# Constants of the start-up laid on another engine, and a key cast held in the order of the text

## The chip, the cores and the metric

The kernel runs on one NeuronCore of a Trainium2 chip. The metric is the device time of one execution in microseconds (us); each median is of a series of 4 to 6 executions (11 or 12 for the kernel before in the experiments). "TensorE", "VectorE", "ScalarE" and "Pool" (GpSimd) appear in profile lines as PE (PEld for its weight loads), DVE, ACT and POOL; SPq is the queue of SyncE, the engine that issues most DMAs (124 of the 151 issues listed for the kernel before). "Granted clock" is the share of full speed that the profile records for TensorE's clock.

## The reference, cut to what matters

A chunked attention feeds a gated feed-forward layer.

```python
# q, k, v: 4 batches, 8 heads, 768 tokens, 64 wide; 8 memory tokens per head
for c in range(24):                         # chunks of 32 tokens
    keys = memory keys + k[32c-16 : 32c+40] # clipped to the sequence
    out[chunk] = softmax(q[chunk] @ keys.T / 8) @ (the same rows of v)
x = out as (3072 tokens, 512)
result = (relu(x @ w_gate) * (x @ w_val)) @ w_out      # 512 -> 1536 -> 512
```

## The kernel before: the parts that matter

The 3072 tokens are worked in eight blocks of 384. Blocks 0 and 1 ("start blocks") are loaded by Pool's queue with a cast on the way and turned on TensorE. Blocks 2 to 7 ("later blocks") are loaded in f32 by SP's queue, cast by VectorE, ScalarE and Pool, and turned by DMA. Each block's feed-forward work consists of twelve "units" (gate and value matmuls, a relu on ScalarE, a product `gvT` on VectorE) and three output units. Attention work of a block is interleaved with the feed-forward units of the block before. In profile lines kf and kn are the loaded and the cast keys, qz the queries, s_ps the scores, v_ps the attention's values, g_ps and vl_ps the gate and value results of the feed-forward.

A scheduler places the instructions of each engine. `pin` keeps an instruction where the text has it among the other pinned ones; an instruction that is not pinned may be moved. The start-up, up to the end of block 1's attention, is chained in the order of the text as well, but only the instructions written there.

```python
pin = tc.keep_in_program_order
...
class LaterBlock(Block):
    def pieces(self, dma):                    # the loads of one block, issued by SP in this order
        def k01():
            ...                               # (memory values first)
            dma(self.kf[16:24, 3], self.mem(mem_k, 0, H, D))
            dma(self.kf[:, 0], self.rows(k, 0, H, self.kbase, 128, D))
        def k12():
            dma(self.kf[0:16, 3], self.rows(k, 0, H, self.kbase + 384, 16, D))
            for t in (1, 2):
                dma(self.kf[:, t], self.rows(k, 0, H, self.kbase + 128 * t, 128, D))
    ...
    def cast_k(self):
        if self.n < 2 + NSTART:
            nc.gpsimd.memset(self.kn[96:128, :, 3], 0.0)          # padding
        view = self.kf.rearrange("p t (a x) d -> p a t (x d)", x=2)
        pin(nc.vector.tensor_copy(self.kn[:, :, 0:3], view[:, :, 0:3]))
        nc.vector.tensor_copy(self.kn[0:24, :, 3], view[0:24, :, 3])   # the tail cast: 24 rows, not pinned
...
# start: first loads, constants by Pool, clearing by ScalarE
b0.load("k", 0); b0.load("q", 0)
...
make_identity(nc, ids["b"])
b0.load("v", 0)
...
lows["first"] = build_low("low_first", NMEM - 16)   # each: memset, two selects, memset, all on Pool
lows["int"] = build_low("low_int", NMEM)
b0.load("k", 4)
...
for u in range(9):                            # block 0's feed-forward, units 0 to 8
    dff[0][u]()
fills = {0: dff[0][9], 1: dff[0][10], 2: dff[0][11]}
start_attention(b1, attention(b1, order0), lambda i: fills.get(i, lambda: warm(2))())
in_text_order(text0)
sp_after(0, w_out_sb[0:1, 0, 0:1])            # SP waits here for the first piece of w_out
for f in b2.pieces(sp):                       # only then are block 2's loads issued
    f()
...
prepare(b2, (hooks, 5), (hooks, 6), (hooks, 7), (hooks, 8))   # b2.cast_k belongs after unit 5 of block 1
```

The softmax here doesn't subtract the row's maximum and nothing guards it: scores larger than these inputs give would overflow.

## Time and profile before

| | before |
|---|---|
| time, median (range) of 4 runs | 265.19 us (264.62 to 265.4) |
| span of the profiled run | 263.3 us |
| TensorE busy | 236.1 us, 90% |
| first gate matmul of block 0 / 1 / 2 (timeline) | 26.44 / 70.94 / 106.68 us |

The page of the kernel before. The first line is busy time and its share of the span; the others give the busy share (or the granted TensorE clock) in tenths of full, for 40 equal slices of 6.6 us.

```profile
PE 236.1 (90%) x1718; PEld 141.7 (54%) x1718; DVE 138.6 (53%) x357; ACT 114.4 (43%) x224; POOL 63.7 (24%) x120
...
PE   5788990398899699999999999999999999999994
...
PEclk9589996579999999999999999999999999999999
```

From the fifteenth slice on TensorE is full. The zero in the seventh slice is a hole. The waits view of the first 60 us says who waited for whom (total, times, longest):

```profile
ACT kb L261 <- DVE kb L257: 15.3, 2, 13.3
...
DVE kn_103 L323 <- DMA kf_99<-in_k_dram: 12.7, 1, 12.7
PE g_ps L431 <- DVE gvT L440: 11.3, 1, 11.3
```

TensorE's 11.3 us and ScalarE's 13.3 us are both waits for VectorE, and VectorE itself waits 12.7 us for a load of keys. The timeline shows the order of events (start, duration, engine, line, operation, destination and source; in brackets the idle time before it and what ended it):

```profile
42.41 0.73 SPq L89 DMA_DIRECT2D here<-w_out_sb  x1
...
44.38 3.37 SPq L89 DMA_DIRECT2D kf_99<-in_k_dram  x4
...
49.38 0.49 DVE L323 CAST kn_103<-kf_99 24x512 bf16<-24x512 f32 x1 [12.71 <-DMA kf_99<-in_k_dram]
49.80 1.00 DVE L440 TENSOR_TENSOR gvT<-vl_ps,g_relu 128x384 f16<-128x384 f32 x2
50.39 1.44 PE L431 MATMUL g_ps<-xT,w_gate_sb 128*128 128x384 f16 x4 [11.26 <-DVE gvT L440]
```

The 24-row tail cast of block 2 stands in front of two products of block 0. Its rows are loaded only after the first piece of w_out is there (42.41 us). VectorE stood for 12.71 us until the cast's rows were there; the two products that the scheduler put behind it start right after it, at 49.80 us. The products read results of TensorE (vl_ps), for which the program has four buffers, shared with g_ps; the next gate matmul waited 11.26 us for a product, and TensorE stopped.

The windows view gives for each stretch its length, busy time and instructions of PE, PEld, DVE, ACT and POOL, then granted clock, DMA share and GB/s. The stretch behind the hole runs at about half clock (0.54 granted):

```profile
39.10:50.40 11.30, 0.04 (x3) 0.06 (x2) 1.02 (x3) 0.00 (x0) 5.57 (x20) 0.62 1.16 212
50.40:55.90 5.50, 5.50 (x28) 2.65 (x28) 2.40 (x5) 2.15 (x5) 0.00 (x0) 0.54 1.08 246
```

The granted clock fell from 1.00 to 0.50 at 41.8 us, 2.7 us after the end of TensorE's last matmul (39.1).

That the tail cast stands so early was the scheduler's choice. In the text it comes right behind the main key cast of the same block, which is pinned. In VectorE's timeline the main cast runs 30 us after its tail, with 35 other instructions of VectorE between them:

```profile
79.48 0.95 DVE L322 CAST kn_103<-kf_99 128x1536 bf16<-128x1536 f32 x1
```

### The profile page before, as it was taken

To read this page: it belongs to the slowest core of one execution; us is meant where nothing else is said; L and a number is where in the kernel's file an instruction comes from. 1 tells how busy PE (TensorE), PEld (TensorE's weight loads), DVE (VectorE), ACT (ScalarE), POOL (GpSimd) and SP (SyncE) were. 2 spreads that over 40 slices of the span, in tenths; PEclk is the share of its full clock that TensorE was granted. 3 is DMA by queue.
4 is the path that set the end of the run, shared out by engine and by line. 5 is a ranking of instruction groups with operands and counts; after the bars stand their busy time and mean duration, and the time that the engine had idled before them with its cause. 6 is when DMAs were issued, how large, how long until landed. Compare 5 with 4: busy or idle time off the path is not lost.

```text
span 263.3 us, 4699 instructions
## 1 busy us (share of the span) xinstructions
PE 236.1 (90%) x1718; PEld 141.7 (54%) x1718; DVE 138.6 (53%) x357; ACT 114.4 (43%) x224; POOL 63.7 (24%) x120
## 2 busy tenths in 40 slices
PE   5788990398899699999999999999999999999994
PEld 3556550165665354556456645664666466546641
DVE  5357920335545842489438934893488258604410
ACT  6436330145535343557246615561565166323321
POOL 8984374315000012134400403052003000000000
PEclk9589996579999999999999999999999999999999
DMA  5599999980006999999969975996699611121012
GB/s 72 72 173 204 204 196 205 249 157 1 2 0 121 232 202 229 229 246 154 165 190 257 140 172 164 248 179 160 171 221 167 171 40 31 32 81 42 0 40 81
DMA packets 96929, 37.55 MB, mean 143 GB/s; under 512 B 78410, under 2 KB 93834, under 8 KB 96906
## 3 DMA queue, kind: packets, MB, share of 16 engines
q1 hardware_dynamic: 85202, 29.85, 53.1%
q0 software_dynamic: 11632, 7.34, 19.3%
q8 instruction: 13, 0.21, 0.3%
q14 instruction: 10, 0.08, 0.1%
q10 hardware_dynamic: 72, 0.07, 0.1%
HBM read 30.43 MB, written 6.29 MB: 139 GB/s over the span
## 4 chain that ended last, share of the span: by engine, by line
PE 75%; DMA 13%; POOL 5%; DVE 2%; issue 2%; ACT 1%; SPq 1%; POOLq 0%; DVEq 0%
PE out_ps L450 24%; PE g_ps L431 21%; PE vl_ps L435 21%; DMA w_gate_sb<-in_moe_w_gate_dram 5%; DMA w_out_sb<-in_moe_w_out_dram 4%; PE s_ps L368 4%; PE o_ps L386 3%; DMA kf_99<-in_k_dram 2%; DMA qT<-qn_105 2%; PE v_ps L282 1%; POOL w_gate_sb L92 1%; SPq L89 1%; POOL w_val_sb L92 1%; POOL qn_105 L92 1%; DVE qz_98 L357 1%
## 5 line engine op out<-in xcount | busy, mean ns | idle before, releaser
L431 PE MATMUL g_ps<-xT,w_gate_sb 128*128 128x384 f16 x384 | 79.5, 330 | 12.0 <-DVE gvT L440 11.3
L440 DVE TENSOR_TENSOR gvT<-vl_ps,g_relu 128x384 f16<-128x384 f32 x96 | 52.9, 554 | 65.9 <-PE vl_ps L435 63.8
L435 PE MATMUL vl_ps<-xT,w_val_sb 128*128 128x384 f16 x384 | 79.3, 329 | 0.1
L438 ACT ACTIVATE g_relu<-g_ps 128x384 f16<-128x384 f32 x96 | 47.0, 490 | 42.8 <-DVE gvT L440 23.7
L450 PE MATMUL out_ps<-w_out_sb,gvT 128*128 128x512 f16 x288 | 64.1, 379 | 0.0
L431 PEld LDWEIGHTS <-w_gate_sb 128*128 128x128 f16 x384 | 36.3, 98 | 31.7 <-issue 13.3
L435 PEld LDWEIGHTS <-w_val_sb 128*128 128x128 f16 x384 | 37.8, 99 | 25.5 <-issue 1.5
L450 PEld LDWEIGHTS <-gvT 128*128 128x128 f16 x288 | 28.0, 98 | 32.0
L453 ACT COPY o_sb<-out_ps 128x512 f32<-128x512 f32 x24 | 14.1, 585 | 51.1 <-PE out_ps L450 50.6
L391 DVE TENSOR_TENSOR x_big<-o_ps,rinv 96x256 f16<-96x256 f32 x64 | 26.5, 417 | 1.5
L368 PE MATMUL s_ps<-qz_97,kb 128*128 128x192 bf16 x64 | 11.5, 258 | 4.1 <-DVE qz_97 L357 2.0
L304 POOL COPY vf_101<-memv 8x512 f32<-8x512 f32 x12 | 7.8, 684 | 23.8 <-DMA memv<-in_mem_v_dram 23.8
L389 DVE RECIPROCAL rinv<-o_ps 96x4 f32<-96x4 f32 x64 | 10.8, 171 | 5.1 <-PE o_ps L386 5.0
L368 PEld LDWEIGHTS <-kb 128*128 128x128 bf16 x128 | 10.6, 100 | 5.0 <-issue 3.0
L368 PE MATMUL s_ps<-qz_98,kb 128*128 128x192 bf16 x64 | 10.8, 244 | 2.0 <-DVE qz_98 L275 0.9
L340 POOL CAST vb_107<-vf_102 128x512 f16<-128x512 f32 x4 | 3.0, 745 | 36.1 <-DMA vf_102<-in_v_dram 36.1
L498 PE MATMUL warm_ps<-idle 128*128 128x256 f16 x38 | 7.9, 337 | 1.2 <-DVE idle L478 1.2
L261 ACT COPY kb<-k_ps 128x240 bf16<-128x240 bf16 x4 | 1.4, 358 | 17.3 <-DVE kb L257 15.3
L323 DVE CAST kn_103<-kf_99 24x512 bf16<-24x512 f32 x3 | 1.3, 421 | 12.7 <-DMA kf_99<-in_k_dram 12.7
L340 POOL CAST vb_108<-vf_102 128x512 f16<-128x512 f32 x4 | 3.1, 772 | 19.4 <-DMA vf_102<-in_v_dram 19.4
L340 POOL CAST vb_109<-vf_102 128x512 f16<-128x512 f32 x4 | 3.0, 743 | 19.2 <-PE vl_ps L435 17.9
L304 POOL COPY vf_102<-memv 8x512 f32<-8x512 f32 x12 | 7.4, 653 | 0.0
(172 smaller groups left out, 234.9 us busy)
## 6 DMA issues: line engine op xcount, KB each, us to landing
out_dram<-o_sb SPq DMA_DIRECT2D x24, 256.0 KB
qf<-in_q_dram SPq DMA_DIRECT2D x6, 768.0 KB
vf_101<-in_v_dram SPq DMA_DIRECT2D x12, 240.0 KB
vf_102<-in_v_dram SPq DMA_DIRECT2D x12, 240.0 KB
kf_99<-in_k_dram SPq DMA_DIRECT2D x9, 256.0 KB
kf_100<-in_k_dram SPq DMA_DIRECT2D x9, 256.0 KB
w_out_sb<-in_moe_w_out_dram POOLq DMA_DIRECT2D x3, 512.0 KB, 11.6
w_gate_sb<-in_moe_w_gate_dram POOLq DMA_DIRECT2D x2, 512.0 KB, 12.0
```

Source lines behind the costliest of these rows:

```text
L304: pin(nc.gpsimd.tensor_copy(self.vf[0:NMEM, j], memv[self.b]))
L340: pin(nc.gpsimd.tensor_copy(self.vb[:, j, :, 0:D], self.vf[:, j]))
L368: nc.tensor.matmul(s_ps[:, i], lhsT=blk.kb[:, 2 * g + i, j, :], rhs=blk.qz[:, 2 * g + i, :, :, 32 * j:32 * j + 32], start=True, stop=not o ...
L389: nc.vector.reciprocal(rinv, o_ps[0:QB, :, D:D + 1])
L391: nc.vector.tensor_tensor(out=x_big[:, 256 * g:256 * g + 256].rearrange("p (h d) -> p h d", h=4), in0=o_ps[0:QB, :, 0:D], in1=rinv_b, op=A ...
L431: nc.tensor.matmul(g_ps, lhsT=w_gate_sb[:, f, 128 * m:128 * m + 128], rhs=blk.xT[:, f, :], start=(f == 0), stop=(f == NFC - 1))
L435: nc.tensor.matmul(vl_ps, lhsT=w_val_sb[:, f, 128 * m:128 * m + 128], rhs=blk.xT[:, f, :], start=(f == 0), stop=(f == NFC - 1))
L438: nc.scalar.activation(g_relu, g_ps, ACT.Relu)
L440: nc.vector.tensor_tensor(out=state["gvT"][:, m].rearrange("p t j c -> p j t c"), in0=vl_ps.rearrange("p (j t c) -> p j t c", j=NJ, t=NT), ...
L450: nc.tensor.matmul(out_ps, lhsT=state["gvT"][:, m, t].rearrange("p j c -> p (j c)"), rhs=w_out_sb[:, m, :], start=(m == 0), stop=(m == NDC ...
L453: nc.scalar.copy(o_sb, out_ps)
L498: nc.tensor.matmul(ps[:, 0:256], lhsT=idle[:, 0:128], rhs=idle, start=True, stop=True)
```

## The change

Its stated intent: start the first loads sooner by taking constants off Pool (VectorE lays the memsets, Pool keeps a few selects between its DMA issues), and hold the key cast and padding of later blocks in the order of the text. The core of the diff:

```diff
-    def build_low(name, first):
-        t = wpool.tile([128, 128], BF16, name=name)
-        nc.gpsimd.memset(t, 0.0)
+    def build_lows(name, first, n, step):          # several masks in one tile, one pair of selects
+        t = wpool.tile([128, n, 128], BF16, name=name)
+        nc.vector.memset(t, 0.0)
 ...
+    def build_ident():                             # memset on VectorE, one select on Pool
 ...
         def cast_k(self):
             if self.n < 2 + NSTART:
-                nc.gpsimd.memset(self.kn[96:128, :, 3], 0.0)
+                pin(nc.vector.memset(self.kn[96:128, :, 3], 0.0))
             view = self.kf.rearrange("p t (a x) d -> p a t (x d)", x=2)
             pin(nc.vector.tensor_copy(self.kn[:, :, 0:3], view[:, :, 0:3]))
-            nc.vector.tensor_copy(self.kn[0:24, :, 3], view[0:24, :, 3])
+            pin(nc.vector.tensor_copy(self.kn[0:24, :, 3], view[0:24, :, 3]))
 ...
-    clear_other_heads(nc.scalar.copy, qz_t[0])     # now two VectorE memsets read as f32
-    b0.cast_mem(nc.vector)
+    b0.cast_mem(nc.scalar.copy)
 ...                                                # b0's second half is loaded earlier,
                                                    # memory rows are issued by SP, not ScalarE
     weights(1024, 1536)
+    clear_other_heads(qz_t[1])
+    lows["last"], = build_lows("low_last", NMEM + 8, 1, 0)
+    sels[1] = build_sel(1, steps)
+    b1.cast_mem(nc.vector.tensor_copy)
     for h0 in (0, 4):                              # block 1's loads now stand behind the selections
         for which in "kqv":
             b1.load(which, h0)
 ...
-    sels[1] = build_sel(1, steps)
-    lows["last"] = build_low("low_last", NMEM + 8)
-    clear_other_heads(nc.vector.tensor_copy, qz_t[1])
-    b1.cast_mem(nc.vector)
```

More of the change, by code (lines that the diff above doesn't have):

```diff
@@ L5 @@
 from concourse import mybir
-from concourse.masks import make_identity
 from concourse._compat import with_exitstack
@@ L128, in build_mask @@
         return mp
-    def build_low(name, first):
-        t = wpool.tile([128, 128], BF16, name=name)
-        nc.gpsimd.memset(t, 0.0)
+    def build_lows(name, first, n, step):
+        t = wpool.tile([128, n, 128], BF16, name=name)
+        nc.vector.memset(t, 0.0)
         for base, mult in ((-first, 1), (first + 55, -1)):
             nc.gpsimd.affine_select(
-                out=t, in_=t, pattern=[[mult, 128]], compare_op=ALU.is_ge,
+                out=t, in_=t, pattern=[[-step * mult, n], [mult, 128]], compare_op=ALU.is_ge,
                 fill=LOW, base=base, channel_multiplier=-32 * mult)
-        nc.gpsimd.memset(t[:, 0:NMEM], 0.0)
-        return t
+        nc.gpsimd.memset(t[:, :, 0:NMEM], 0.0)
+        return [t[:, i] for i in range(n)]
     def build_chunks():
         t = wpool.tile([128, 2, NT, 32], BF16, name="chunks")
-        nc.gpsimd.memset(t, 1.0)
+        nc.vector.memset(t, 1.0)
         for base, mult in ((0, 1), (31, -1)):
@@ L148, in build_chunks @@
                 fill=0.0, base=base, channel_multiplier=-32 * mult)
+        return t
+    def build_ident():
+        t = wpool.tile([128, 128], BF16, name="ident_b")
+        nc.vector.memset(t, 0.0)
+        nc.gpsimd.affine_select(out=t, in_=t, pattern=[[-1, 128]], compare_op=ALU.not_equal,
+                                fill=1.0, base=0, channel_multiplier=1)
         return t
@@ L169, in shifted @@
                            ap=[steps.ap[0], [-1, KR]] + mids + [[1, BAND]])
-        nc.vector.memset(sel[:, :, :, 0:NMEM], 0.0)
+        sl = sel[:, :, :, 0:NMEM]
+        nc.vector.memset(sl, 0.0)
         nc.vector.tensor_copy(sel[:, :, first:first + 3, NMEM:], shifted(rel[first], [[QB, 3]]))
         nc.vector.tensor_copy(sel[:, :, odd, NMEM:], shifted(rel[odd], []))
-        sl = sel[:, :, :, 0:NMEM]
         nc.gpsimd.affine_select(
@@ L226, in load_mem, with cast_mem @@
                 dma(dst, self.mem(m, 0, H, KR * D))
-        def cast_mem(self, engine):
+        def cast_mem(self, copy):
             for dst, src in zip((self.kc, self.vc), self.mems):
-                engine.tensor_copy(dst[0:TOK0], src)
+                copy(dst[0:TOK0], src)
         def keys(self, h):
@@ L478 @@
     nc.vector.memset(idle, 0.0)
-    b0.load("k", 0)
-    b0.load("q", 0)
-    for b in (b0, b1):
-        b.load_mem(nc.scalar.dma_start)
-    scratch = wpool.tile([1, 1], F32, name="scratch")
-    nc.scalar.activation(scratch, zeros[0:1], ACT.Exp)
-    def clear(op, t, ps, x):
-        z = zeros[ps]
-        op(t[ps, :, x], bass.AP(tensor=z.tensor, offset=z.offset, ap=[z.ap[0], [0, HP], [0, NT], [0, 128]]))
-    def clear_other_heads(op, t):
-        clear(op, t, slice(0, D), 1)
-        clear(op, t, slice(D, 128), 0)
-    clear_other_heads(nc.scalar.copy, qz_t[0])
     def warm(n):
@@ L500, with clear_other_heads @@
     warm(16)
-    ids["b"] = wpool.tile([128, 128], BF16, name="ident_b")
-    make_identity(nc, ids["b"])
-    b0.load("v", 0)
+    b0.load("k", 0)
+    for b in (b0, b1):
+        b.load_mem(nc.sync.dma_start)
+    scratch = wpool.tile([1, 1], F32, name="scratch")
+    nc.scalar.activation(scratch, zeros[0:1], ACT.Exp)
+    ids["b"] = build_ident()
+    b0.load("q", 0)
+    b0.load("v", 0)
+    b0.load("k", 4)
+    b0.cast_mem(nc.scalar.copy)
+    ids["chunks"] = build_chunks()
+    lows["first"], lows["int"] = build_lows("low_first", NMEM - 16, 2, 16)
+    b0.load("q", 4)
+    def clear_other_heads(t):
+        nc.vector.memset(t[0:D, :, 1].bitcast(F32), 0.0)
+        nc.vector.memset(t[D:128, :, 0].bitcast(F32), 0.0)
     steps = build_steps()
+    clear_other_heads(qz_t[0])
+    b0.load("v", 4)
+    ids["h"] = wpool.tile([128, 128], F16, name="ident_h")
+    nc.vector.tensor_copy(ids["h"], ids["b"])
     for t in vb_t:
@@ L508 @@
         nc.vector.memset(t[:, :, QB:128], 0.0)
-    b0.cast_mem(nc.vector)
-    ids["chunks"] = build_chunks()
-    lows["first"] = build_low("low_first", NMEM - 16)
-    lows["int"] = build_low("low_int", NMEM)
-    b0.load("k", 4)
-    ids["h"] = wpool.tile([128, 128], F16, name="ident_h")
-    nc.vector.tensor_copy(ids["h"], ids["b"])
     order = [(j, g) for j in range(NJ) for g in range(2)]
@@ L563, in start_attention, with selections @@
         fill(6)
-    def rest_of_b0():
-        b0.load("q", 4)
+    def selections():
         sels[0] = build_sel(0, steps)
-        b0.load("v", 4)
         weights(0, 256)
         weights(256, 512)
-    start_attention(b0, attention(b0, order0), lambda i: (warm(2), rest_of_b0() if i == 1 else None))
+    start_attention(b0, attention(b0, order0), lambda i: (warm(2), selections() if i == 1 else None))
     weights(512, 1024)
     weights(1024, 1536)
+    clear_other_heads(qz_t[1])
+    lows["last"], = build_lows("low_last", NMEM + 8, 1, 0)
+    sels[1] = build_sel(1, steps)
+    b1.cast_mem(nc.vector.tensor_copy)
     for h0 in (0, 4):
```

## The prediction

> **What bounds the kernel now.** From 106.7 us to the end TensorE is the limit: the windows view gives it 152.4 us of work in 156.6, and its longest wait there is 0.6 us. The idle time lies before. The largest piece is one hole: the timeline has TensorE idle for 11.26 us up to 50.39 us, waiting for a VectorE product (gvT). The cause is one instruction ahead of it in VectorE's stream: the 24-row tail of block 2's key cast (kn_103 from kf_99), which waits 12.71 us for a key load. That load is issued only after the first w_out piece lands (42.4 us); the cast starts at 49.4 and is not needed until about 80. It was not pinned, and the scheduler put it after the seventh gvT of block 0. The hole costs twice: the granted clock is 0.54 from 50.4 to 55.9, so four gate matmuls took 1.44 us instead of 0.65. [...]
>
> **What the change does.**
> 1. Tail cast and padding are pinned. In the changed order the cast stands behind six gvT of block 1. The hole closes: -11.3 us. The stretch 50.4 to 55.9 then runs at full clock; adding up its chain (four matmul groups of 0.65, a query turn of 0.5) I estimate 3.4 us instead of 5.5: -2.1 us.
> 2. Pool's start. Pool loses the identity memset (1.21 us), chunks memset (0.28), two low memsets (0.20 each) and two selects (0.29 to 0.36 each). VectorE gains these memsets (0.1 to 0.3 each) and head clearing (about 1.6, an estimate from the 232-word memset's 0.25); ScalarE gains the memory casts and loses its clearing (2.93). Weights are issued earlier (about 11 instead of 12.4 us). Queries are issued later (3.5 instead of 2.2) but should land about when they did (7.9). TensorE's start hangs on the first key load (issued 1.37, landed 6.8), unchanged; block 0's attention is then a chain of small steps, not of loads. Value: -0.3 us, uncertain by 1.
> 3. Block 1's loads now stand behind selections that need VectorE after block 0's attention: issued near 28 us instead of 18.9. Weights occupy the queue until about 31 anyway, and block 1 first needs its keys at 38.5: no cost.
> 4. The tail cast now delays block 2's key turn by about 0.5 us, where TensorE already waited 2.0 us (scores for qz_97, 88.0); two output matmuls now go ahead of them. Net +0.2. Later blocks: +0.3 at most.
>
> **Sum.** 265.08 - 11.3 - 2.1 - 0.3 + 0.4 = 251.8; I put 251.5 us, range 249.0 to 254.5 (8 in 10). Faster by over 2%: 0.97; within 2%: 0.02; slower: 0.01.
>
> **What would show it.** No TensorE wait over 3 us after 10 us, clock 1.00 from about 17 us on; the tail cast at about 65 us without a wait for a load; block 1's feed-forward from about 57 instead of 70.9 us; first weight issue near 11; first scores still near 10.4.
>
> **What would make it wrong.** A second wait under the hole: block 1's late loads arriving after 39 us, or block 2's keys after about 65. ScalarE's casts of memory rows (about 4 us) delaying its first key copies. Pinned casts holding up gvT in every later block.

The sum came to 251.8 us, put at 251.5, and its -2.1 us for the half clock rests on the trace of the kernel before (granted clock 0.54, a gate group of 1.44 us). Durations of work that the kernel before does not contain are estimates: VectorE's memsets there took 0.06 to 0.25 us, and ScalarE's clearing of 3072 elements a row took 2.93 us, which gives 3.9 for casts of 2x2048 (measured after: 1.90 and 1.89 us).

## The result, and the profile after

The changed kernel takes 250.7 us (median of 4 runs, 250.43 to 252.49) against 265.19 us. The ratio is 0.9471, with a 95% interval of 0.9425 to 0.9518. A ratio here is always the mean time of one kernel's runs over that of the other's of the same rounds, so it is not quite the ratio of the medians quoted.

| | before | after |
|---|---|---|
| time, median | 265.19 us | 250.7 us |
| span of the profiled run | 263.3 us | 249.1 us |
| first gate matmul of block 0 | 26.44 | 26.12 |
| block 0's to block 1's first gate matmul | 44.50 us | 30.82 us |
| block 1's to block 2's first gate matmul | 35.74 us | 35.68 us |
| from there to the end | 156.62 us | 156.48 us |

The differences of the three stages come from the same timeline starts as in the table before. One stage holds 13.68 of the 14.2 us. The page after, the same lines:

```profile
PE 234.6 (94%) x1718; PEld 140.8 (57%) x1718; DVE 138.2 (55%) x363; ACT 115.2 (46%) x224; POOL 60.0 (24%) x110
...
PE   5788999889979999999999999999999999999994
...
PEclk9999999999999999999999999999999999999999
```

TensorE's busy time is the same within 1.5 us; its idle time fell. The waits view of TensorE, whole span:

```profile
PE s_ps L374 <- DVE qz_97 L363: 1.8, 1, 1.8
PE s_ps L374 <- DVE qz_97 L281: 1.7, 2, 1.0
PE k_ps L250 <- POOL low_first L135: 1.7, 1, 1.7
```

The longest wait is now 1.8 us, the one before block 2's first scores. The timeline where the hole was, and where the tail cast went:

```profile
38.52 0.82 PE L437 MATMUL g_ps<-xT,w_gate_sb 128*128 128x384 f16 x4
...
44.61 0.70 SPq L88 DMA_DIRECT2D here<-w_out_sb  x1
...
46.23 4.62 SPq L88 DMA_DIRECT2D kf_99<-in_k_dram  x4
...
65.98 0.96 DVE L328 CAST kn_103<-kf_99 128x1536 bf16<-128x1536 f32 x1
66.85 0.41 DVE L329 CAST kn_103<-kf_99 24x512 bf16<-24x512 f32 x1
```

The gate group that stood at 50.39 us now starts at 38.52 and takes 0.82 instead of 1.44 us. The loads did not come sooner: SP's wait for w_out ended at 44.61 us, 2.2 us later than before. The keys were late in both; after the change nothing stands behind them.

The windows view of the stretch where the hole was and of the one behind it:

```profile
39.10:50.40 11.30, 10.07 (x116) 7.05 (x115) 6.22 (x16) 6.33 (x15) 4.05 (x17) 1.00 1.20 206
50.40:55.90 5.50, 4.57 (x62) 3.87 (x61) 3.56 (x12) 3.17 (x8) 0.95 (x2) 1.00 0.78 214
```

The clock row needs care: it reads 1.00 from the first microsecond after the change (the trace holds no clock record before 13.94 us), yet the first key turn (16 transposes at 6.49 us) took 0.97 us where the same turn takes 0.59 at 38.00 us, and the query turn behind it (7.93 us) took 0.85. In the kernel before a query turn took 0.85 us at 7.90, where the granted clock was 0.50 (8 to 10 us), and 0.53 at 16.57, where it was 1.00. So I take it that the array was at half clock at the start after the change too, and trust the durations of equal matmuls more than this row.

### The profile page after: what moved, and what is told of

Read it like the earlier page. It is cut to its first block, busy times and chain, and to the rows that moved or that the text cites. A ratio compares the mean times of both kernels' runs of the same rounds, so it can differ in the third digit from the quotient of the medians.

```text
span 249.1 us, 4702 instructions
## 1 busy us (share of the span) xinstructions
PE 234.6 (94%) x1718; PEld 140.8 (57%) x1718; DVE 138.2 (55%) x363; ACT 115.2 (46%) x224; POOL 60.0 (24%) x110
## 4 chain that ended last, share of the span: by engine, by line
PE 85%; DVE 5%; ACT 3%; POOL 2%; DMA 2%; issue 2%; POOLq 0%; DVEq 0%; ACTq 0%
PE out_ps L456 25%; PE g_ps L437 23%; PE vl_ps L441 23%; PE s_ps L374 5%; PE v_ps L288 3%; PE o_ps L392 3%; DMA qT<-qn_105 2%; PE s_ps L378 1%; DVE x_big L397 1%; DVE kb L263 1%; PE k_ps L250 1%; DVE gvT L446 1%; POOL kn_103 L91 1%; ACT qz_98 L280 1%; ACT qz_97 L280 1%
## 5 line engine op out<-in xcount | busy, mean ns | idle before, releaser
L437 PE MATMUL g_ps<-xT,w_gate_sb 128*128 128x384 f16 x384 | 78.2, 326 | 0.7 <-ACT xT L411 0.7
L441 PE MATMUL vl_ps<-xT,w_val_sb 128*128 128x384 f16 x384 | 78.4, 326 | 0.0
L310 POOL COPY vf_101<-memv 8x512 f32<-8x512 f32 x12 | 7.5, 662 | 26.2 <-DMA memv<-in_mem_v_dram 19.5
L382 ACT ACTIVATE ex_110<-s_ps 128x384 f16<-128x384 f32 x8 | 3.9, 491 | 7.1 <-PE s_ps L374 4.9
L310 POOL COPY vf_102<-memv 8x512 f32<-8x512 f32 x12 | 7.1, 628 | 0.0
L356 DVE COPY kb<-kT 128x1440 bf16<-128x1440 bf16 x6 | 3.2, 536 | 7.0 <-DMA kT<-kn_103 4.5
```

The costliest lines, as they stand in the source:

```text
L310: pin(nc.gpsimd.tensor_copy(self.vf[0:NMEM, j], memv[self.b]))
L437: nc.tensor.matmul(g_ps, lhsT=w_gate_sb[:, f, 128 * m:128 * m + 128], rhs=blk.xT[:, f, :], start=(f == 0), stop=(f == NFC - 1))
L441: nc.tensor.matmul(vl_ps, lhsT=w_val_sb[:, f, 128 * m:128 * m + 128], rhs=blk.xT[:, f, :], start=(f == 0), stop=(f == NFC - 1))
```

## The experiments

Theory: the one unpinned tail cast stood ahead of products that TensorE needed, and cost 11.3 us of waiting plus about 2 us of half clock (0.54 granted over the 5.5 us behind the hole). First rival: the start, with constants off Pool and earlier issues, earned the time. Second rival: block 2's loads as such were the limit, and moving the cast only moves the wait. All kernels below gave correct results.

### Only the pins, only the tail's pin, and only the start

`pins_only` is the kernel before with both pins; `tail_pin_only` with the tail's alone; `start_only` is the changed kernel with both taken back.

```diff
 # pins_only, on the kernel before (tail_pin_only: the second pair of lines alone)
-                nc.gpsimd.memset(self.kn[96:128, :, 3], 0.0)
+                pin(nc.vector.memset(self.kn[96:128, :, 3], 0.0))
-            nc.vector.tensor_copy(self.kn[0:24, :, 3], view[0:24, :, 3])
+            pin(nc.vector.tensor_copy(self.kn[0:24, :, 3], view[0:24, :, 3]))
 # start_only: the reverse of these, on the changed kernel
```

> The kernel before with nothing but the two pinned instructions of the key cast (tail cast, and padding memset on VectorE). Theory (the unpinned tail cast at VectorE's head blocks TensorE, and the idle array then runs at half clock): 251.8 us, 13.4 below before, no TensorE wait over 3 us after 10 us. Rival (the earlier issues at the start earn the time): about 264.5, hole still there.

> The changed kernel with the two instructions unpinned again, all start changes kept. The order listing puts the tail cast behind the eleventh gvT of block 0, later than before (seventh). Theory: a smaller hole at a later place, about 5 to 6 us of TensorE idle ending near 51 us when the tail rows land, plus some 2 us of half clock: 258.5 us (256.5 to 260.5). Rival (the start earns the time): about 251.

> The kernel before with only the tail cast pinned; the padding memset stays unpinned on Pool. Theory (the tail cast alone makes the hole): the same as with both pins, ratio to before 0.952 within 0.005, no TensorE wait over 3 us after 10 us. Rival (the padding memset on Pool has a share): clearly above 0.957.

> The changed kernel once more, as the mark of this call: 250.5 to 252.5 us, as its two earlier series.

| run | median | ratio to before (95%) | block 0's to block 1's first gate matmul |
|---|---|---|---|
| before, same chip | 265.81 us | 1 | 44.50 us (the profile above) |
| `pins_only` | 253.11 | 0.952 (0.9475 to 0.9565) | 30.82 us |
| `tail_pin_only` | 252.16 | 0.9491 (0.9472 to 0.951) | 30.83 us |
| `start_only` | 259.4 | 0.9772 (0.9745 to 0.9799) | 39.50 us |
| `after_third` (the changed kernel) | 251.46 | 0.947 (0.9443 to 0.9498) | 30.82 us |

The tail's pin alone shortens the stage to what the whole change does, within 0.01 us. Where the hole was, TensorE now works, and the tail cast stands without a wait behind the main one:

```profile
37.66 0.82 PE L431 MATMUL g_ps<-xT,w_gate_sb 128*128 128x384 f16 x4
...
65.49 0.41 DVE L323 CAST kn<-kf 24x512 bf16<-24x512 f32 x1
```

The median of `tail_pin_only` is 0.7 us above that of the changed kernel, but the intervals overlap, so the rest of the change is not resolved from nothing. The first rival falls as the source of the gain.

`start_only` was predicted at 258.5 and took 259.4 us: the scheduler placed the unpinned cast in a different place (behind the eleventh product), and the hole moved with it. Its timeline:

```profile
51.18 0.53 DVE L329 CAST kn<-kf 24x512 bf16<-24x512 f32 x1 [9.39 <-DMA kf<-in_k_dram]
51.63 0.67 DVE L291 CAST vb<-v_ps 128x512 f16<-128x512 f32 x1
...
52.35 0.38 PE L392 MATMUL o_ps<-vb,ex 128*128 128x66 f16 x4 [6.94 <-DVE vb L291]
52.54 1.47 PE L437 MATMUL g_ps<-xT,w_gate_sb 128*128 128x384 f16 x4
```

The wait of TensorE is 6.94 us instead of 11.26, because it had more work to do before it ran into the cast; the half clock behind it is there again (1.47 us for a gate group, granted clock 0.50 from 50.4 to 55.9 us). The start's changes alone had pushed the cast later by four products, as a side effect of where the scheduler then put it; that is most of the gain `start_only` shows: the stage gives 5.00 (39.50 instead of 44.50 us) of the 6.1 us between the two profiled spans. The other 1.05 us is an earlier first gate matmul (25.39 instead of 26.44), which lies within the scatter of the start (see "Why the prediction was right").

`pins_only` was 1.3 us above its mark. Its profile has the same 30.82 us stage; the excess lies elsewhere: its start was late (block 0's first gate matmul at 27.46 us), and the stage from block 1's to block 2's first gate matmul took 37.32 instead of 35.7 us, because the array ran at half clock there for 3.4 us (0.78 and 0.88 granted over the two windows of 5 us below). The granted clock falls at 77.8 us, 1.5 us after the only wait of TensorE in that stretch, 1.8 us before block 2's scores; that this wait caused it is inferred from the order. Its windows and timeline there:

```profile
75.00:80.00 5.00, 3.76 (x24) 1.93 (x24) 3.87 (x11) 1.85 (x4) 0.00 (x0) 0.78 1.02 235
80.00:85.00 5.00, 5.00 (x41) 2.78 (x40) 1.88 (x9) 1.76 (x4) 0.61 (x1) 0.88 1.03 197
```

```profile
76.24 0.49 PE L368 MATMUL s_ps<-qz,kb 128*128 128x192 bf16 x4 [1.77 <-DVE qz L357]
...
78.27 3.11 PE L450 MATMUL out_ps<-w_out_sb,gvT 128*128 128x512 f16 x7
```

Seven output matmuls took 3.11 us; the same seven took 1.67 after the change, behind an equally long wait (1.78 us). In `tail_pin_only` that stage was as long (37.26 us), behind waits of 0.66 and 1.17 us; in the kernel before, a wait of 1.99 us at the same scores was followed by full clock (1.00 granted from 55.5 us to the end). What decides is not shown. For comparing kernels it is scatter of some 1.6 us.

### The wait without the half clock

`hole_filled` keeps the cast where it was and gives TensorE needless matmuls in the hole.

```diff
-    fills = {0: dff[0][9], 1: dff[0][10], 2: dff[0][11]}
+    def busy(n):                       # writes a score tile that nobody reads
+        ps = sps.tile([128, 2, 2, NT, 32], F32, name="s_ps")
+        for _ in range(n):
+            nc.tensor.matmul(ps[:, 0], lhsT=idle[:, 0:128], rhs=idle[:, 0:192], start=True, stop=True)
+    def busy_and_unit():
+        busy(125)
+        dff[0][9]()
+    fills = {0: busy_and_unit, 1: dff[0][10], 2: dff[0][11]}
```

> The kernel before with 125 needless matmuls (192 columns, about 10 us) on TensorE where the hole is; the tail cast stays where it was. It separates the two costs of the hole. Theory (11.3 us of waiting and 2.1 us of half clock afterwards): the wait stays, the stretch behind it takes 3.4 instead of 5.5 us, total 263.1 us. If the half clock costs nothing: 265.2. If the clock were the larger part: under 260.

Measured: 263.6 us, ratio 0.9924 (0.9893 to 0.9955). The timeline:

```profile
37.89 10.49 PE L620 MATMUL s_ps<-idle 128*128 128x192 f16 x125
...
48.48 0.41 DVE L323 CAST kn<-kf 24x512 bf16<-24x512 f32 x1 [12.98 <-DMA kf<-in_k_dram]
...
49.42 0.81 PE L431 MATMUL g_ps<-xT,w_gate_sb 128*128 128x384 f16 x4 [1.04 <-DVE gvT L440]
```

The cast still waits 12.98 us, but the gate group behind it takes 0.81 instead of 1.44 us. The stage took 42.61 instead of 44.50 us: the half clock cost 1.89 us, and the other 11.79 of the 13.68 us are left for the wait. So the half clock is measured on its own, and the wait by subtraction. (In this run block 0's first gate matmul came 1.06 us earlier than in the profile of before and the cast 0.90 us earlier, so up to 0.2 us of the wait may belong to the clock.) Kept busy, the array did not drop: the granted clock was 1.00 from 39.1 to 50.4 and from 50.4 to 55.9 us, where the kernel before had 0.62 and 0.54.

### The same hole closed from the other end

`tail_rows_early` leaves the cast unpinned and loads the 24 rows of block 2 at the start, ahead of SP's wait for w_out.

```diff
+            def tail():                                    # taken out of k01 and k12
+                dma(self.kf[16:24, 3], self.mem(mem_k, 0, H, D))
+                dma(self.kf[0:16, 3], self.rows(k, 0, H, self.kbase + 384, 16, D))
+            if self.n > 2: ...                             # later blocks: first of their pieces
+            else: tail()                                   # block 2: at once
 ...
+    b2_pieces = b2.pieces(sp)
     sp_after(0, w_out_sb[0:1, 0, 0:1])
-    for f in b2.pieces(sp):
+    for f in b2_pieces:
```

> The kernel before, tail cast unpinned, but the 24 tail rows of block 2's keys are loaded at the start, ahead of the wait for w_out. The scheduler then places the cast in block 0's attention, with its data there. Theory (only the cast's wait for its rows matters, whichever end is moved): about 251.8 us, no hole. Rival (the load traffic of block 2 as a whole has to be waited for): 260 or more, the wait turning up at the main key cast.

Measured: 252.18 us, ratio 0.9486 (0.9462 to 0.9511), stage 30.92 us; no wait of TensorE above 2.2 us. The cast stands early and waits for nothing:

```profile
17.54 0.38 DVE L332 CAST kn<-kf 24x512 bf16<-24x512 f32 x1
```

The remaining key loads of block 2 came as late as ever and nothing waited for them. So the second rival falls too: what counted was that one instruction's data came after its turn, and either end could be moved.

### Block 1's loads, later by the change

After the change block 1's loads stand behind two Pool selections that need VectorE. `loads_first` puts them back in front.

```diff
-    clear_other_heads(qz_t[1])
-    lows["last"], = build_lows("low_last", NMEM + 8, 1, 0)
-    sels[1] = build_sel(1, steps)
-    b1.cast_mem(nc.vector.tensor_copy)
     for h0 in (0, 4):
         ...                                      # block 1's loads and w_out
+    clear_other_heads(qz_t[1])
+    ...                                          # the same four, here
```

> The changed kernel again, as the mark for the runs of the same call: 250.7 us.

> The changed kernel with block 1's loads issued before the selections that wait for VectorE, as they stood before the change. The changed kernel's queue runs dry between 29 and 32 us because these loads are issued at 30.5. Theory (off the critical path): the dry stretch goes, w_out and block 2's keys land 3 to 4 us earlier, the time stays within 0.4 us of the changed kernel. Rival (the late loads cost part of the gain): over 0.8 us faster.

Measured on one chip: 252.17 us for the changed kernel (ratio 0.9487, 0.9449 to 0.9526) and 251.4 for `loads_first` (0.9463, 0.9437 to 0.9488). The medians differ by 0.8 us, more than the 0.4 expected; the intervals overlap, and the stage from block 0 to block 1 is 30.82 us in both profiles. (The same reordering puts `best` 0.85 us ahead of `scores_later` below. No stage of the profiles shows such a gain, but a small one is not excluded.) The effect on the queue is plain. Windows of the changed kernel (first series), then of `loads_first`; the last two columns are DMA share and GB/s:

```profile
30.00:32.00 2.00, 2.00 (x14) 1.17 (x12) 1.95 (x5) 0.55 (x2) 2.00 (x5) 1.00 0.14 21
```

```profile
30.00:32.00 2.00, 2.00 (x14) 1.22 (x13) 1.86 (x4) 0.55 (x2) 0.24 (x1) 1.00 1.51 190
```

The queue runs nearly dry for some 3 us after the change, and SP's wait for w_out ends at 40.51 us in `loads_first` instead of 44.61, 46.83 and 45.01 us in the three profiles of the changed kernel. TensorE is busy for all 2.00 us of that window in both, so the gap in the loads was no loss to it.

The same pair shows why Pool was so late. Pool's timeline in the changed kernel, then in `loads_first`:

```profile
27.20 1.96 POOL L135 TENSOR_SCALAR_AFFINE_SELECT low_last<-low_last 128x128 bf16<-128x128 bf16 x2 [10.11 <-DVE sel_499 L177]
29.21 1.06 POOL L138 MEMSET low_last<- 128x8 bf16 x1
29.31 1.19 POOL L180 TENSOR_SCALAR_AFFINE_SELECT sel_499<-sel_499 114x128 f16<-114x128 f16 x1
```

```profile
33.40 0.67 POOL L135 TENSOR_SCALAR_AFFINE_SELECT low_last<-low_last 128x128 bf16<-128x128 bf16 x2
34.12 0.10 POOL L138 MEMSET low_last<- 128x8 bf16 x1
34.22 0.41 POOL L180 TENSOR_SCALAR_AFFINE_SELECT sel<-sel 114x128 f16<-114x128 f16 x1
```

From the first start to the last end these four instructions take 3.3 us in one place and 1.2 in the other. In the first place VectorE runs two casts of f32 memory rows (1.21 and 1.30 us, 27.79 to 30.23). In the other place no such cast runs beside them (there they end at 29.92 us). So the 128x8 memset took 1.06 us beside a cast and 0.10 without. What makes it slower is not shown, and the notes of `prof` call spans on Pool rough.

It also puts a number of the prediction in doubt. The identity's memset and select cost Pool 1.21 and 1.15 us before, and I booked the memset as Pool's own work. The timeline of before has VectorE's memory casts beside them for nearly all of that time:

```profile
2.79 1.24 DVE L230 CAST kn_103<-kf_99 2x2048 bf16<-2x2048 f32 x1 [0.61 <-DMA kf_99<-in_mem_k_dram]
2.97 1.21 POOL masks.py:197 MEMSET ident_b<- 128x128 bf16 x1
...
3.96 1.29 DVE L230 CAST vc_122<-vf_101 2x2048 f16<-2x2048 f32 x1
4.25 1.15 POOL masks.py:199 TENSOR_SCALAR_AFFINE_SELECT ident_b<-ident_b 128x128 bf16<-128x128 bf16 x1
```

After the change, with those casts on ScalarE, the select takes 0.30 us:

```profile
2.29 0.30 POOL L153 TENSOR_SCALAR_AFFINE_SELECT ident_b<-ident_b 128x128 bf16<-128x128 bf16 x1
```

### Warming the array longer

```diff
-    warm(16)
+    warm(36)
```

> The changed kernel with 36 instead of 16 warming matmuls at the start, so that TensorE is busy until the first keys land (about 6.5 us). In the changed kernel the first key turn takes 0.97 us against 0.59 later, so the array ran at half clock there although the clock row reads 1.00. If the wait before the first keys is what drops the clock: 16 key turns in 0.6 us, sixteen value matmuls in 1.9 instead of 2.6, about 1.0 us less (249.7). If block 0's attention is paced by the other engines: within 0.3 us.

Measured: 252.51 us, ratio 0.9513 (0.9482 to 0.9544) against 0.9487 of the changed kernel in the same call: no gain. The first key turn did take 0.59 us, but block 0's first scores started at 10.10 us (10.37 after the change), and its first gate matmul at 26.01 (26.12). The run doesn't settle what the half clock costs at the start, because the array did not stay at full clock: the granted clock reads 0.50 from 12 to 14 us, after another wait of TensorE before the first scores (1.66 us; that this wait brought it down is not shown), and the sixteen matmuls for attention values (v_ps) that were to take 1.9 us took 2.85. After the change, then here:

```profile
12.98 2.38 PE L288 MATMUL v_ps<-vc_122,sel_246 114*128 114x256 f16 x16
```

```profile
12.40 2.85 PE L288 MATMUL v_ps<-vc,sel 114*128 114x256 f16 x16
```

### Following the next wait, and a version that beats both

The longest wait left was the 1.8 us before block 2's scores. `prepare_earlier` places block 2's casts and turns earlier.

```diff
-    prepare(b2, (hooks, 5), (hooks, 6), (hooks, 7), (hooks, 8))
+    prepare(b2, (hooks, 3), (hooks, 4), (hooks, 7), (hooks, 7))
```

> The changed kernel with block 2's key and query casts, turns and bands placed earlier in the text (units 3, 4, 7, 7 instead of 5, 6, 7, 8). After the hole is gone, the longest TensorE wait past 10 us is 1.8 us for qz_97 before block 2's first scores. If it is a matter of placing only: wait gone, 1.8 us less than the changed kernel, about 248.9. If something else comes behind it: less than 0.8 us gained.

Measured: 252.09 us, ratio 0.9487, the same as the changed kernel; a miss. The wait was still 2.0 us:

```profile
71.88 1.12 DVE L363 COPY qz<-qT 64x1536 bf16<-64x1536 bf16 x2 [0.56 <-DMA qT<-qn]
...
73.05 0.33 PE L374 MATMUL s_ps<-qz,kb 128*128 128x192 bf16 x2 [2.01 <-DVE qz L363]
```

The queries were ready about 2 us earlier in the stage, but the scheduler, seeing them earlier, also moved the scores ahead in TensorE's stream (from behind the second output matmul to the middle of unit 10). `scores_later` therefore places the scores later too, and `best` adds the order of loads of `loads_first`.

```diff
-    prepare(b2, (hooks, 5), (hooks, 6), (hooks, 7), (hooks, 8))
+    prepare(b2, (hooks, 2), (hooks, 3), (hooks, 7), (hooks, 8))
-        [(10, 11), (11, 12), (12, 13), (12, 13), (13, 14), (13, 14), (14, 15), (14, 15)])
+        [(12, 13), (12, 13), (12, 13), (12, 13), (13, 14), (13, 14), (14, 15), (14, 15)])
```

> The changed kernel with block 2's casts and turns placed at units 2 and 3, and its first scores placed two units later in the text (12 instead of 10), so that in the order listing they stand behind all twelve feed-forward units. In the run with only the casts earlier the scheduler moved the scores forward by as much and the wait stayed (2.0 us). Theory (it is where the scores stand in TensorE's stream against the landing of the query turn): wait under 0.5 us, 1.5 us less than the changed kernel of this call. If the work behind it (the last turns of block 2's rows) then waits instead: no gain.

> The kernel of scores_later with block 1's loads issued before the selections. Off the critical path: the same as scores_later within 0.5 us, 1.5 us below the changed kernel; the queue does not run dry at 29 to 33 us.

Measured: `scores_later` 250.37 us, ratio 0.9427 (0.9404 to 0.945); `best` 249.52 us, 0.9392 (0.9369 to 0.9414); the changed kernel in the same call 251.46, 0.947. In both the scores no longer wait at that place, and the stage from block 1 to block 2 takes 33.84 and 33.63 us instead of 35.69. About 0.9 us of wait for these queries is left in the profile of `scores_later`, at one later place; so it gained 1.1 us and not the 1.5 expected. `best` is the fastest kernel measured, some 0.8% below the changed one. Its lead over `scores_later`, 0.85 us where at most 0.5 was expected, is not explained: the intervals touch, the stages agree within 0.5 us, and its profiled run differs mainly by an earlier first gate matmul (25.33 against 26.45 us). That comes from earlier first scores (9.49 against 10.23 us) and shorter v_ps matmuls behind them (2.48 against 2.85 us), both ahead of the point where the orders of the two part (16.85 us). In the profiles it is scatter of the start; whether it is in the medians is open.

## Why the prediction was right

- **The hole and its half clock.** Predicted -11.3 and -2.1 us, together -13.4. Measured: the stage fell from 44.50 to 30.82 us, 13.68; `hole_filled` splits that into 11.79 and 1.89 (each good to about 0.2). `tail_pin_only` shows that the tail's pin alone does it, `tail_rows_early` that the late rows were what it waited for.
- **The start.** Predicted -0.3, uncertain by 1 us. In the five profiles with the old start (before, `pins_only`, `tail_pin_only`, `hole_filled`, `tail_rows_early`) block 0's first gate matmul starts at 25.25 to 27.46 us, mean 26.26; in the eight with the new one and sixteen warming matmuls at 25.33 to 27.67, mean 26.14. The difference is a twentieth of the scatter. The first weight was issued at 11.11 us, as predicted (11), and first scores began at 10.37 (10.4); it bought nothing that these profiles resolve, so the -0.3 is not confirmed, and that the total fits is luck in this term. The scatter has a source that the prediction left out. In all thirteen of these profiles the first gate matmul follows 13.35 to 13.38 us after the sum of two figures: when the first scores start (9.45 to 10.80 us) and how long the sixteen v_ps matmuls behind them take (2.02 to 3.50 us, against 1.91 for the same group in block 1, 57.70 us in the kernel before, at full clock). So this group stands on the start's chain, and it was slowed by the half clock (in the kernel before 2.62 us, granted clock 0.50 from 12 to 14 us); it isn't only "small steps". The step "the query load should land about when it did" held in the first profile (the query turn starts at 7.93 against 7.90 us), but in `after_again` the query turn waited 1.1 us for it.
- **Block 1's loads.** "No cost" was right in time. The reason given was partly wrong: issue was at 30.46 us instead of 28, because Pool's selections took 3.3 us beside VectorE's casts, and the weights had landed by then, so the queue did run dry. It cost nothing only because TensorE needed those keys at 38.00 us.
- **Block 2's key turn.** Predicted +0.2, measured -0.06 us (35.74 to 35.68). The key turn did come later, as predicted (10.35 instead of 9.56 us after block 1's first gate matmul), but the wait before the scores was 1.78 instead of 1.99 us.
- **Later blocks.** Predicted at most +0.3; the last stage went from 156.62 to 156.48 us in the first pair of profiles, and 157.2 in another profile of the changed kernel. Below what can be resolved.
- **Total.** 251.5 predicted, 250.7 us measured in the first series; the two later series of the same kernel gave 252.17 and 251.46.

## What to carry to other kernels

When an engine stops for a load, as VectorE did here for 12.71 us, ask what that instruction is doing there: a cheap instruction (0.49 us here) placed ahead of its data can hold up what stands behind it (TensorE for 11.26 us here), and pinning it to where it is needed may be worth more than any tuning of the work itself. Count the half clock behind an idle stretch of TensorE as a cost of its own (1.9 us here, behind 11.3). And test a change of several parts one part at a time: here one pinned line gave all that could be resolved of a rewrite of the start.
